# First loads put in one sequence on one DMA queue, with the last weight chunks moved to a second queue behind a wait

## The chip, the cores and the metric

The kernel runs on one core of one Trainium2 chip. The metric is the device time of one execution in microseconds (us). Executions of one kernel differ here by about 0.5% without any change, so medians are given with their range, and ratios with a 95% interval. A ratio is the mean time of one kernel's fast runs over that of the other's in the same rounds, so it is not quite the ratio of the medians beside it. The profile counts a "span" from the first to the last instruction, about 1.3 us less than the time of the same execution.

## The reference, cut to what matters

```python
x = A_x                                           # [1, 2048, 640], bf16
g = sigmoid((x * gate_w).sum(-1, keepdims=True))
qkv = x @ wqkv                                    # wqkv [640, 1920]: q, k, v of 640 columns each
pq, pk = phi(q), phi(k)                           # phi(t) = where(t > 0, t + 1, exp(t)) + 1e-6
a = linear_attention(pq, pk, v) @ wo
b = (gelu(x @ w_gate) * (x @ w_up)) @ w_down
return g * a + (1 - g) * b
```

The argument touches only the very first work: Q and K of the first row tiles of x (128 rows each). A projection sums over 640 input columns in five chunks of 128, so it needs x transposed and the five chunks of the weights wk and wq, 160 KB each.

## The kernel before

DMAs are issued from two queues, SyncE's ("sp") and ScalarE's ("act"). Tiles 0 and 1 of x are loaded plainly and transposed on TensorE; tiles 2 to 15 come by DMA transposes on SyncE's queue. The first of these waits until wk chunk 4 has landed.

```python
load_x(0)
load_wk(0)
load_x(1, "act")
load_wk(1)
load_wk(3)
# ...
load_wk(2, "act")
load_wk(4, "act")
# ... (gate weights, "act")
for k in range(KC):                       # KC = 5
    load_wq(k, ("sp", "act")[k % 2])
# ...
for i in range(NXN, NT):                  # tiles 2 to 15
    load_xT(i, after=([r_wk[4]] if i == NXN else ()))
# ... bulk loads of x and of the other weights, same queue
```

TensorE's order: warming matmuls on constants, transposes `T(tile, chunks, bank)`, then K steps `KM(n, [chunk])` and Q steps `QM(n, [chunk])` of both tiles, then `KQ(i)`, the joint K and Q projection of tiles 2 to 15.

```python
warm(5, 512); warm(1, 128)
T(0, [0], 7); T(0, [1, 2, 3, 4], 6)
warm(6, 128)
KM(0, [0])
T(1, [0], 7); T(1, [1, 2, 3, 4], 6)
warm(3, 128)
KM(1, [0])
for k in (1, 2, 3):
    KM(0, [k]); KM(1, [k])
gate_col()
for k in (4,):
    KM(0, [k]); KM(1, [k])
# ... Q of tiles 0 and 1 chunk by chunk, phi of all four results
for i in range(2, NT):
    KQ(i)
```

Of the kernel before, what the change touches and what calls it, by code (L numbers as in the profile page):

```python
# [16 lines left out]
KC = D // 128  # L17
# [6 lines left out]
NXN = 2  # L24
# [137 lines left out]
def bass_gated_mix__linear_attn_block__geglu_ffn__prompt_kernel(  # L162
# [63 lines left out]
    with (  # L226
# [8 lines left out]
        with contextlib.ExitStack() as stack:  # L235
            dma_sems = [stack.enter_context(nc.semaphore("s_in%d" % i)) for i in range(n_dma_in)]

            P = _Plan(["pe", "act", "dve", "pool", "sp"])
# [9 lines left out]
            def new_dma_key():  # L248
                k = "in%d" % dma_next[0]
                dma_next[0] += 1  # L250
                return k

            def v16(o, n):
                return pool[:, o:o + n]
# [14 lines left out]
            wq = wkq[:, :, 640:1281]  # L269
# [30 lines left out]
            gw_sb = v16(O_GW, 128)  # L300
# [8 lines left out]
            r_wk = [P.sb("wk%d" % k, R_WK + k * WW, R_WK + k * WW + 640) for k in range(KC)]  # L309
            r_wq = [P.sb("wq%d" % k, R_WK + k * WW + 640, R_WK + k * WW + 1280) for k in range(KC)]  # L310
# [26 lines left out]
            r_gw = P.res("gw")  # L337

            def dma_in(dst, src, writes, reads=(), eng="sp"):
                P.op(eng, lambda e, dst=dst, src=src: e.dma_start(dst, src),  # L340
                     reads=reads, writes=writes, dma=new_dma_key())
# [3 lines left out]
            def load_x(i, eng="sp"):  # L345
                dma_in(x_aug[:, i, 0:640], A_x[0, i * 128:(i + 1) * 128, :], [r_xn[i]], eng=eng)

            def load_wk(k, eng="sp"):
                dma_in(wk[:, k, :], A_wqkv[k * 128:(k + 1) * 128, 640:1280], [r_wk[k]], eng=eng)

            def load_wq(k, eng="sp"):
                dma_in(wq[:, k, 0:640], A_wqkv[k * 128:(k + 1) * 128, 0:640], [r_wq[k]], eng=eng)


            P.op("act", lambda e: e.dma_start(touch[0:16, 0:4], A_wqkv[0:128:8, 640:644]),
                 writes=[P.res("touch")], dma=new_dma_key())
            load_x(0)
            load_wk(0)
            load_x(1, "act")
            load_wk(1)  # L360
            load_wk(3)

            zero = nc.const_aps.tensor(0.0, (128, 1), F32)
            P.op("act", lambda e: e.activation(eg[:, 0:1], zero, ACT.Exp), writes=[r_eg[0]])
            load_wk(2, "act")
            load_wk(4, "act")
            P.op("dve", lambda e: e.memset(gw_sb, 0.0), writes=[r_gw])
            dma_in(gw_sb[0:5, :], gate_w.rearrange("(k p) -> k p", p=128), [r_gw], eng="act")
            for k in range(KC):
                load_wq(k, ("sp", "act")[k % 2])  # L370

            def load_xT(i, after=()):
                P.op("sp", lambda e: e.dma_start_transpose(xT[:, :, i * 128:(i + 1) * 128],
                                                           A_x[0, i * 128:(i + 1) * 128, :]),
                     reads=list(after), writes=[r_xT[i]], dma=new_dma_key())

            for i in range(NXN, NT):
                load_xT(i, after=([r_wk[4]] if i == NXN else ()))
            dma_in(x_aug[:, NXN:8, 0:640],
                   A_x[0, NXN * 128:8 * 128, :].rearrange("(i p) w -> p i w", p=128), r_xn[NXN:8])  # L380
            dma_in(x_aug[:, 8:NT, 0:640],
# [4 lines left out]
            for c in range(NHC):  # L386
# [9 lines left out]
                 reads=[r_ones], writes=[r_ident])  # L396
# [16 lines left out]
            def warm(count, n):  # L413
                def fn(e):
                    last = None
                    for w in range(count):
                        last = e.matmul(ps[:, 4, 0:n], one_l, one_r[:, 0:n], start=True, stop=True)
                    return last
                P.op("pe", fn, writes=[bank[4]])
# [4 lines left out]
            def slot(n):  # L424
                return SLOTS[n % 4]

            def T(i, ks, tb):
                def fn(e):
                    last = None
                    for n, k in enumerate(ks):  # L430
                        last = e.transpose(psb[:, tb, n * 128:(n + 1) * 128],
                                           x_aug[:, i, k * 128:(k + 1) * 128], ident)
                    return last
                P.op("pe", fn, reads=[r_xn[i], r_ident], writes=[bank[tb]])
                P.op("dve", lambda e: e.tensor_copy(
                    xT[:, ks[0]:ks[-1] + 1, i * 128:(i + 1) * 128],
                    psb[:, tb, 0:len(ks) * 128].rearrange("p (k s) -> p k s", k=len(ks))),
                    reads=[bank[tb]], writes=[r_xTa[i] if ks[0] == 0 else r_xT[i]])
# [4 lines left out]
            def KM(n, ks):  # L443
                i = seq[n][1]
                b0, b1 = slot(n)

                def fn(e):
                    last = None
                    for k in ks:
                        lhs = xT[:, k, i * 128:(i + 1) * 128]  # L450
                        e.matmul(ps[:, b0, :], lhs, wk[:, k, 0:512], start=(k == 0), stop=(k == KC - 1))  # L451
                        last = e.matmul(ps[:, b1, 0:128], lhs, wk[:, k, 512:640],
                                        start=(k == 0), stop=(k == KC - 1))
                    return last
                P.op("pe", fn, reads=[r_xTa[i] if i < NXN and ks == [0] else r_xT[i]] + [r_wk[k] for k in ks],
                     writes=[bank[b0], bank[b1]])
# [37 lines left out]
            def gate_col():  # L494

                P.op("pe", lambda e: e.matmul(ps[:, 7, 0:5], gw_sb, ident[:, 0:5], start=True, stop=True),
                     reads=[r_gw, r_ident], writes=[bank[7]])
                P.op("dve", lambda e: e.tensor_copy(wq[:, :, 640:641], ps[:, 7, 0:5].unsqueeze(2)),
                     reads=[bank[7]], writes=[r_gcol])
# [4 lines left out]
            warm(1, 128)  # L504
            T(0, [0], 7)
            T(0, [1, 2, 3, 4], 6)
            warm(6, 128)
            KM(0, [0])
            T(1, [0], 7)
            T(1, [1, 2, 3, 4], 6)  # L510
            warm(3, 128)
            KM(1, [0])
            for k in (1, 2, 3):
                KM(0, [k])
                KM(1, [k])
            gate_col()
            for k in (4,):
                KM(0, [k])
                KM(1, [k])
            for n in range(4):  # L520
# [42 lines left out]
            for i in range(2, NT):  # L563
                KQ(i)
                if i == 4:
                    late_constants()
            P.op("dve", lambda e: e.tensor_scalar(gg, eg, 0.5, 0.5, ALU.mult, ALU.add),
                 reads=r_eg, writes=[r_g])
            P.op("dve", lambda e: e.tensor_scalar(omg, eg, -0.5, 0.5, ALU.mult, ALU.add),
                 reads=r_eg, writes=[r_omg])  # L570
# [7 lines left out]
                 reads=[r_omg], writes=[r_od], dma=new_dma_key())  # L578
# [44 lines left out]
            def ME(g):  # L623
# [6 lines left out]
                for c in cs:  # L630
# [8 lines left out]
                 reads=r_pk[0:2], writes=[r_tmp[0]])  # L639
            for i in range(2, NT):  # L640
                P.op("dve", lambda e, i=i: e.tensor_tensor(zacc, zacc, pk[i], ALU.add),  # L641
                     reads=[r_tmp[0], r_pk[i]], writes=[r_tmp[0]])
# [283 lines left out]
```

## Time and profile before

| | before |
|---|---|
| time, median of 6 runs | 273.72 us (273.44 to 274.68) |
| span of the profiled execution | 272.2 us |
| first K step / first Q step / joint projection starts | 4.38 / 7.67 / 10.39 us |
| TensorE busy | 267.9 us, 98% |

The row to read first is TensorE's: it has work in 98% of the span, and it is not interrupted once the joint projection runs. The start of that projection is therefore the number to follow. The rest of the program takes 261.8 us from there to the end (272.2 - 10.39).

### The profile page before, as it was taken

The numbers are of one execution on the slowest core, as the hardware profiler recorded it, in microseconds if no ns is written. First come the engines' busy times: TensorE is split into PE (matmuls) and PEld (weight loads), VectorE is DVE, ScalarE is ACT, GpSimd is POOL, SyncE is SP. The second block draws the span as 40 slices with busy tenths as digits, with TensorE's granted clock in tenths as the row PEclk, the third lists the DMA queues.
The fourth block names the chain that finished last, engine by engine and source line by source line (L and its number), as shares of the span: only waits on it lengthen the run. The fifth ranks groups of instructions, "written<-read, shape, count | busy, mean of one in ns | idle before, by whom it ended". The sixth has DMA issues, their size and how long they took to land.

```text
span 272.2 us, 3426 instructions
## 1 busy us (share of the span) xinstructions
PE 267.9 (98%) x1343; PEld 128.1 (47%) x1369; DVE 141.8 (52%) x251; ACT 75.9 (28%) x132; POOL 30.0 (11%) x28
## 2 busy tenths in 40 slices
PE   8999999999999999999999999999999999999997
PEld 4555555544445444444444444444444444444444
DVE  2689898997333335999999999634110000000200
ACT  2555555210422453332222232224011122121021
POOL 5000000003140002242332421000000000000000
PEclk9999999999999999999999999999999999999999
DMA  6776999500300011612221221272031110110211
GB/s 219 176 114 124 349 402 384 119 2 19 61 16 2 23 50 51 200 28 48 27 48 30 43 50 25 60 229 96 5 79 37 41 39 19 39 41 19 58 58 41
DMA packets 42208, 23.61 MB, mean 87 GB/s; under 512 B 31567, under 2 KB 40783, under 8 KB 42063
## 3 DMA queue, kind: packets, MB, share of 16 engines
q1 hardware_dynamic: 41429, 22.56, 30.5%
q10 hardware_dynamic: 762, 0.82, 0.8%
q8 instruction: 11, 0.18, 0.3%
q14 instruction: 6, 0.05, 0.1%
HBM read 13.83 MB, written 2.63 MB: 60 GB/s over the span
## 4 chain that ended last, share of the span: by engine, by line
PE 95%; DVE 2%; DMA 1%; issue 1%; ACT 1%; SPq 0%; DVEq 0%; ACTq 0%
PE ps L697 41%; PE ps L861 23%; PE ps L536 12%; PE ps L593 6%; PE ps L840 4%; PE ps L808 2%; PE ps L675 2%; PE ps L596 2%; DMA pool<-in_A_wqkv_dram 1%; PE ps L451 1%; PE ps L821 1%; PE ps L466 1%; DVE pool L490 1%; PE ps L718 1%; DVE pool L555 1%
## 5 line engine op out<-in xcount | busy, mean ns | idle before, releaser
L697 PE MATMUL ps<-pool 128*128 128x512 bf16 x510 | 113.0, 379 | 0.5
L697 PEld LDWEIGHTS ps<-pool 128*128 128x128 bf16 x520 | 50.4, 98 | 60.1
L861 PE MATMUL ps<-pool 128*128 128x512 bf16 (+2 forms) x300 | 62.4, 367 | 0.3
L703 ACT ACTIVATE pool<-ps 128x512 f32<-128x512 f32 x52 | 31.0, 597 | 73.1 <-PE ps L697 73.1
L705 DVE TENSOR_TENSOR pool<-ps,pool 128x512 bf16<-128x512 f32 x52 | 34.6, 689 | 31.7 <-PE ps L697 30.4
L861 PEld LDWEIGHTS ps<-pool 128*128 128x128 bf16 x306 | 29.1, 98 | 33.5 <-issue 0.4
L536 PE MATMUL ps<-pool 128*128 128x512 bf16 (+1 forms) x206 | 37.9, 344 | 0.2
L844 DVE TENSOR_TENSOR pool<-ps,pool 128x512 bf16<-128x512 f32 x4 | 2.8, 692 | 61.5 <-PE ps L840 61.5
L751 POOL TENSOR_TENSOR pool<-pool 128x640 f32<-128x640 bf16 x16 | 22.5, 1406 | 72.8 <-DVE pool L753 65.9
L868 ACT ACTIVATE pool<-ps,pool 128x512 bf16<-128x512 f32 (+1 forms) x16 | 10.9, 680 | 68.6 <-PE ps L861 68.6
L536 PEld LDWEIGHTS ps<-pool 128*128 128x128 bf16 x210 | 20.5, 98 | 17.5
L555 DVE SCALAR_TENSOR_TENSOR pool<-ps,pool 128x128 bf16<-128x128 f32 (+2 forms) x42 | 25.3, 603 | 2.4
L546 ACT ACTIVATE pool<-ps 128x640 bf16<-128x640 f32 x28 | 19.7, 703 | 18.1 <-DVE pool L555 10.6
L593 PE MATMUL ps<-pool 128*128 128x512 bf16 x76 | 19.2, 380 | 0.1
L761 DVE TENSOR_TENSOR pool<-pool 128x640 bf16<-128x640 bf16 x16 | 13.2, 825 | 0.6
L759 DVE TENSOR_SCALAR pool<-pool 128x32 f32<-128x32 f32 x16 | 12.8, 803 | 0.6
L753 DVE TENSOR_REDUCE pool<-pool 128x32 f32<-128x640 f32 x16 | 12.9, 809 | 0.0
L641 DVE TENSOR_TENSOR pool<-pool 128x640 f32<-128x640 f32 x14 | 11.6, 826 | 0.5
L840 PE MATMUL ps<-pool 128*128 128x512 bf16 x51 | 11.5, 380 | 0.1
L643 POOL PARTITION_ALL_REDUCE pool<-pool x1 | 4.0, 3971 | 60.7 <-DVE pool L641 60.7
L593 PEld LDWEIGHTS ps<-pool 128*128 128x128 bf16 x78 | 6.9, 98 | 7.2
L552 DVE TENSOR_SCALAR pool<-pool 128x640 bf16<-128x640 bf16 x28 | 9.1, 327 | 1.8 <-ACT pool L546 0.4
(70 smaller groups left out, 105.0 us busy)
## 6 DMA issues: line engine op xcount, KB each, us to landing
out_dram<-pool SPq DMA_DIRECT2D x19, 128.0 KB, 1.7
pool<-in_B_w_gate_dram SPq DMA_DIRECT2D x1, 2080.0 KB, 14.2
pool<-in_B_w_up_dram SPq DMA_DIRECT2D x1, 2080.0 KB, 18.8
pool<-in_A_x_dram SPq DMA_DIRECT2D x1, 1280.0 KB, 8.7
pool<-in_B_w_down_dram SPq DMA_DIRECT2D x1, 1120.0 KB, 6.1
pool<-omg_row SPq DMA_DIRECT2D x1, 1024.0 KB, 4.8
pool<-in_A_wqkv_dram SPq DMA_DIRECT2D x6, 160.0 KB, 4.4
pool<-in_A_x_dram SPq DMA_DIRECT2D x1, 960.0 KB, 5.8
```

The source lines that it names most:

```text
L536: last = e.matmul(ps[:, b + p, 0:c1 - c0], xT[:, k, i * 128:(i + 1) * 128], wkq[:, k, c0:c1], start=(k == 0), stop=(k == KC - 1))
L546: P.op("act", lambda e: e.activation(e_buf[m], ps_flat[:, o:o + 640], ACT.Exp), reads=banks, writes=[r_e[m]])
L555: P.op("dve", lambda e, c0=c0, c1=c1: e.scalar_tensor_tensor(dst[:, c0:c1], ps_flat[:, o + c0:o + c1], 1.0 + EPS, e_buf[m][:, c0:c1], ALU. ...
L593: last = e.matmul(ps[:, b, :], pk[i][:, c * 128:(c + 1) * 128], x_aug[:, i, 0:512], start=(i == 0), stop=(i == NT - 1))
L697: last = e.matmul(ps[:, b, :], w[:, k, fc * 128:(fc + 1) * 128], xT[:, k, j * 512:(j + 1) * 512], start=(k == 0), stop=(k == KC - 1))
L703: P.op("act", lambda e: e.activation(ge[n], ps[:, gb, :], ACT.Gelu_apprx_tanh), reads=[bank[gb]], writes=[r_ge[n]])
L705: P.op("dve", lambda e: e.tensor_tensor(hT[fc][:, j * 512:(j + 1) * 512], ps[:, ub, :], ge[n], ALU.mult), reads=[bank[ub], r_ge[n]], write ...
L751: P.op("pool", lambda e: e.tensor_tensor(tmp[n], pq[i], z_b, ALU.mult), reads=[r_pq[i], r_zb], writes=[r_tmp[n]])
L753: P.op("dve", lambda e: e.tensor_reduce(den[n], tmp[n].rearrange("p (h d) -> p h d", h=32), AX.X, ALU.add), reads=[r_tmp[n]], writes=[r_de ...
L761: P.op("dve", lambda e: e.tensor_tensor(pq[i].rearrange("p (h d) -> p h d", h=32), pq[i].rearrange("p (h d) -> p h d", h=32), den[n].unsqu ...
L840: last = e.matmul(ps[:, b, :], wd[:, fc, 512:640], hT[fc][:, j * 512:(j + 1) * 512], start=False, stop=(fc == NFC - 2), skip_group_check=True)
L861: last = e.matmul(ps[:, pb, 0:c1 - c0], lhs, rhs, start=False, stop=(q == len(rows) - 1), skip_group_check=True)
```

## The change

The intent: give the early loads a fixed order, so that each K chunk arrives when it is wanted and nothing unneeded shares the DMA engines with it. All first loads go on SyncE's queue; wq chunks 2 to 4 are issued by ScalarE, but only when wk chunk 2 is in. The wait ahead of the transposes is dropped. TensorE transposes both tiles before K begins.

```diff
-            load_x(0)
-            load_wk(0)
-            load_x(1, "act")
-            load_wk(1)
-            load_wk(3)
+            load_x(0)
+            load_x(1)
+            for k in range(KC):
+                load_wk(k)
 ...
-            load_wk(2, "act")
-            load_wk(4, "act")
-            (gate weights, now second on ScalarE's queue)
-            for k in range(KC):
-                load_wq(k, ("sp", "act")[k % 2])
+            load_wq(0)
+            load_wq(1)
+            for k in (2, 3, 4):
+                load_wq(k, "act", after=[r_wk[2]])
 ...
-                load_xT(i, after=([r_wk[4]] if i == NXN else ()))
+                load_xT(i)
 ...
-            warm(6, 128)
-            KM(0, [0])
+            warm(2, 128)
             T(1, [0], 7)
-            T(1, [1, 2, 3, 4], 6)
-            warm(3, 128)
-            KM(1, [0])
-            for k in (1, 2, 3): ...   gate_col()   for k in (4,): ...
+            T(1, [1, 2, 3, 4], 5)
+            warm(4, 128)
+            for k in range(KC):
+                if k == 3:
+                    gate_col()
                 KM(0, [k])
                 KM(1, [k])
```

More of the change, by code (lines that the diff above doesn't have):

```diff
@@ L349, in load_wk, with load_wq @@
                 dma_in(wk[:, k, :], A_wqkv[k * 128:(k + 1) * 128, 640:1280], [r_wk[k]], eng=eng)
-            def load_wq(k, eng="sp"):
-                dma_in(wq[:, k, 0:640], A_wqkv[k * 128:(k + 1) * 128, 0:640], [r_wq[k]], eng=eng)
+            def load_wq(k, eng="sp", after=()):
+                dma_in(wq[:, k, 0:640], A_wqkv[k * 128:(k + 1) * 128, 0:640], [r_wq[k]], reads=after, eng=eng)
             P.op("act", lambda e: e.dma_start(touch[0:16, 0:4], A_wqkv[0:128:8, 640:644]),
                  writes=[P.res("touch")], dma=new_dma_key())
+            P.op("dve", lambda e: e.memset(gw_sb, 0.0), writes=[r_gw])
+            dma_in(gw_sb[0:5, :], gate_w.rearrange("(k p) -> k p", p=128), [r_gw], eng="act")
             load_x(0)
-            load_wk(0)
-            load_x(1, "act")
-            load_wk(1)
-            load_wk(3)
+            load_x(1)
+            for k in range(KC):
+                load_wk(k)
             zero = nc.const_aps.tensor(0.0, (128, 1), F32)
             P.op("act", lambda e: e.activation(eg[:, 0:1], zero, ACT.Exp), writes=[r_eg[0]])
-            load_wk(2, "act")
-            load_wk(4, "act")
-            P.op("dve", lambda e: e.memset(gw_sb, 0.0), writes=[r_gw])
-            dma_in(gw_sb[0:5, :], gate_w.rearrange("(k p) -> k p", p=128), [r_gw], eng="act")
-            for k in range(KC):
-                load_wq(k, ("sp", "act")[k % 2])
+            load_wq(0)
+            load_wq(1)
+            for k in (2, 3, 4):
+                load_wq(k, "act", after=[r_wk[2]])
             def load_xT(i, after=()):
@@ L506, in bass_gated_mix__linear_attn_block__geglu_ffn__prompt_kernel @@
             T(0, [1, 2, 3, 4], 6)
-            warm(6, 128)
-            KM(0, [0])
+            warm(2, 128)
             T(1, [0], 7)
-            T(1, [1, 2, 3, 4], 6)
-            warm(3, 128)
-            KM(1, [0])
-            for k in (1, 2, 3):
-                KM(0, [k])
-                KM(1, [k])
-            gate_col()
-            for k in (4,):
+            T(1, [1, 2, 3, 4], 5)
[3 more added lines that the diff above has]
+                    gate_col()
                 KM(0, [k])
```

## The prediction

> **What bounds the kernel now.** I read the page first, then the timeline of the first 18 us engine by engine, then the waits of that stretch, then each load's time to landing one window at a time.
>
> ```profile
> span 272.2 us, 3426 instructions
> PE 267.9 (98%) x1343; PEld 128.1 (47%) x1369; DVE 141.8 (52%) x251; ACT 75.9 (28%) x132; POOL 30.0 (11%) x28
> PE 95%; DVE 2%; DMA 1%; issue 1%; ACT 1%; SPq 0%; DVEq 0%; ACTq 0%
> ```
>
> The busy line and the chain that ended last say the same: TensorE sets the end, and it is free for only 272.2 - 267.9 = 4.3 us of the whole span. The change touches only the first ten microseconds, so all it can do is let TensorE's long unbroken stretch begin earlier or later. The question is where that stretch begins. The timeline of TensorE (start, length, engine, line, form, count, idle before):
>
> ```profile
> 0.82 2.40 PE L417 MATMUL ps<-const-bfloat16-1.0 128*128 128x512 bf16 x6 [0.82 <-PEq L911]
> 3.02 0.74 PE L431 MATMUL ps<-pool 128*128 128x128 bf16 x5
> 3.55 0.62 PE L417 MATMUL ps<-const-bfloat16-1.0 128*128 128x128 bf16 x6
> 4.38 0.38 PE L451 MATMUL ps<-pool 128*128 128x512 bf16 x1 [0.21 <-DMA pool<-in_A_wqkv_dram]
> 4.64 0.44 PE L431 MATMUL ps<-pool 128*128 128x128 bf16 x5
> 4.92 0.34 PE L417 MATMUL ps<-const-bfloat16-1.0 128*128 128x128 bf16 x3
> 5.18 0.39 PE L451 MATMUL ps<-pool 128*128 128x512 bf16 x1
> 5.46 0.38 PE L451 MATMUL ps<-pool 128*128 128x512 bf16 x1
> 5.74 0.38 PE L451 MATMUL ps<-pool 128*128 128x512 bf16 x1
> 7.67 0.38 PE L466 MATMUL ps<-pool 128*128 128x512 bf16 x1
> 10.39 7.85 PE L536 MATMUL ps<-pool 128*128 128x512 bf16 x40
> ```
>
> L417 is warming on constants, L431 the transposes of x tiles 0 and 1, L451 the K projection of these tiles, L466 their Q projection, L536 the joint K and Q projection of tiles 2 to 15. From 5.46 on nothing is free: a step of one tile and one chunk (512 and 128 columns) repeats every 0.27 us (5.46 to 5.74). Nine records of L466 appear where ten instructions were issued, so the small hole near 8.2 is a missing record. L536 needs 2.71 us a tile; ScalarE's first read of each comes at that interval:
>
> ```profile
> 15.46 0.70 ACT L546 ACTIVATE pool<-ps 128x640 bf16<-128x640 f32 x1 [0.45 <-PE ps L536]
> 18.17 0.70 ACT L546 ACTIVATE pool<-ps 128x640 bf16<-128x640 f32 x1 [0.46 <-PE ps L536]
> ```
>
> So the useful stretch starts at 5.46, with chunk 1, and what held it there is a load: the weight-load row at 5.45 has 0.16 us idle put down to the weight DMA. The loads themselves:
>
> ```profile
> 0.79 0.41 SPq L340 DMA_DIRECT2D pool<-in_A_x_dram  x1
> 1.26 2.78 SPq L340 DMA_DIRECT2D pool<-in_A_wqkv_dram  x6
> 6.51 19.01 SPq L373 DMA_TRANSPOSE pool<-in_A_x_dram  x14
> 1.23 0.45 ACTq L340 DMA_DIRECT2D pool<-in_A_x_dram  x1
> 1.78 0.87 ACTq L340 DMA_DIRECT2D pool<-in_A_wqkv_dram  x2
> SPq L373 <- DMA pool<-in_A_wqkv_dram: 2.5, 1, 2.5
> ```
>
> SyncE issues every (4.04 - 1.26)/6 = 0.46 us. Adding the times to landing, window by window, to the times of issue: x0 0.79+2.2 = 3.0; wk0 1.26+3.0 = 4.25; x1 1.23+3.2 = 4.4; wk1 1.71+3.7 = 5.4; wk2 1.78+3.8 = 5.6; wk3 2.18+4.1 = 6.25; wk4 2.19+4.3 = 6.5; wq0 7.4; wq1 7.8; wq2 8.25; wq4 8.9; wq3 8.95. After x1, nine loads take 4.5 us: one 160 KB load per 0.50 us. Two queues feed one supply, and wk1 waits in it beside wk2, which nobody needs yet.
>
> **What the Trainium skill says.** "DMA: Bandwidth & Descriptors", section "Issuing engines are not separate DMA queues": transfers issued from ScalarE and SyncE run on the same 16 DMA engines and interleave, and a second issuer saves only issue time. The trace agrees: the spacing of 0.50 us with two issuers is hardly longer than one issuer's 0.46 us. So one issuer should lose almost no supply, and order becomes controllable. The same page, "DMA Transpose (X-bar)" and its rules: a transpose beside ordinary loads needs no serializing, so dropping the wait for wk4 is safe; whether it costs bandwidth the page does not say for this mix. "TensorE: Matmul & The Clock Gate", section "What's actually happening": the array runs at half rate until about 3.4 us of activity, run-variably. Here the five 512-column warming matmuls take about 0.43 us each (2.40 us for five and a small one, less the overlap of ends), the step at 5.46 shows 0.21 us from L451 to L452, and by 4.38 the array is fast.
>
> **The change part by part.**
>
> Order of loads. All of x0, x1, wk0 to wk4, wq0, wq1 go at 0.46 us from 0.79: issues at 0.79, 1.26, 1.72, 2.18, 2.65, 3.11, 3.57, 4.04, 4.50. I estimate landings from before: the second load on SyncE's queue landed at 4.25 while sharing with x1, so alone about 3.6; three loads were in by 4.4 with parts of two others, so wk0 at about 4.1; then 0.50 each: wk1 4.6, wk2 5.1, wk3 5.6, wk4 6.1, wq0 6.6, wq1 7.1.
>
> TensorE's start. Both tiles are now transposed before any K step, which needs x1 (3.6). After the first transposes and two warming matmuls TensorE is at about 3.75; five transposes at about 0.09 us and four warming matmuls at 0.07 bring it to about 4.5. VectorE has by then copied chunk 0 of both tiles (0.23 us each, its queue being free at 4.2). wk0 is there. So K starts at 4.5, and with two tiles a chunk takes 0.55 us against one load per 0.50 us: chunks 1 to 4 are wanted at 5.05, 5.6, 6.15, 6.7 and are there 0.45 us earlier or more.
>
> Before, K chunk 1 began at 5.46; now at 4.5 + 0.55 = 5.05. Gain 0.41 us. The gate column is one matmul as before, only a chunk earlier, and its load, now second on ScalarE's queue instead of fifth, is early enough: 0.
>
> Q. ScalarE blocks until wk2 lands (5.1), then issues three loads at 0.44: 5.15, 5.6, 6.05. Nothing else is asked of ScalarE until the end of K near 7.25, so blocking costs 0. Q wants its chunks at 7.3, 7.85, 8.4, 8.9, 9.45. wq0 and wq1 have 0.7 us to spare. wq2 to wq4 compete with SyncE's transposes, now issued from about 4.97 instead of 6.51. By 0.50 us each after wq1 they come at 7.6, 8.1, 8.6; if transposes take a third of the supply (estimate), 7.8, 8.5, 9.2. Enough, but only by 0.25 us at the end.
>
> Transposes. The first of them came 3.7 us after issue; behind wq1 it should be there by about 9.2, and tile 2 is wanted at 10.39 - 0.41 = 9.98. They go on at 1.36 us each against 2.71 us of TensorE, so they stay ahead; the 1.5 us by which all later loads move forward wins nothing.
>
> Warming: nine small matmuls become six; they lie before the start and cost nothing beyond what is counted above.
>
> Sum: 0.41 us less, of which I keep 0.35 because the margin at wq4 is thin. 273.87 - 0.35 is 273.5 us.
>
> **Rivals.** One: the transposes take the supply from wq2 to wq4 and Q waits. For it: the margin of 0.25 us and the removed wait, which was there to keep transposes behind the weights. Against: they queue behind wq1 on SyncE, and ScalarE's loads are on their own queue. It would eat 0.2 to 0.6 us: 273.7 to 274.1. Two: one queue supplies the start more slowly (x1 near 4.1 rather than 3.6), and TensorE idles before the first K step. K then starts at 4.8 to 5.0, the gain falls to nothing: 273.8. Three: with four fewer warming matmuls between the two sets of transposes, and both sets of transposes ahead of K, the clock opens later. Up to 3 us of K steps at half rate would cost 1.5 us: 275. Against: TensorE is as busy as before from 0.82 on, and it was fast at 4.38; I give it one chance in twelve. Four: the phi work of VectorE takes the place as bound; its loop repeats with TensorE's at 2.71 us and moves along with it, so no.
>
> **Range and chances.** Three runs of before spread over 1.15 us, more than the effect. The range is the effect (-0.6 to +0.2) and half that spread: 272.8 to 274.4. A change of 2% is 5.5 us, more than TensorE's whole idle time, so faster is next to excluded; slower would need a stall that nothing here shows.
>
> **What would show it.** The first L451 near 4.5 with no idle time before it; both L451 tiles without a break; the first L466 near 7.25 (before 7.67); the first L536 near 9.97 (before 10.39); transposes issued from 5.0. An idle stretch on TensorE put down to weights during L466 is rival one; idle time before the first L451 is rival two; L451 steps of 0.5 us are rival three. The span otherwise unchanged from L536 on. If L536 starts over 0.3 us earlier and the time does not fall, noise or a later wait decides, and the argument is wrong that everything after simply shifts.

## The result, and the profile after

| | before | after |
|---|---|---|
| median of 6 runs | 273.72 us (273.44 to 274.68) | 276.66 us (275.92 to 277.55) |
| ratio of fast runs | 1 | 1.0099 (1.0071 to 1.0128) |
| span of the profiled execution | 272.2 | 274.7 |
| first K / first Q / joint projection | 4.38 / 7.67 / 10.39 | 4.83 / 8.44 / 12.94 |

The kernel became slower by 1.0%, some 2.9 us; the prediction was 0.35 us faster. The profiled execution is the fastest of the six, so it shows the smallest loss, 2.5 us. The page's own lines of the changed kernel are these:

```profile
span 274.7 us, 3446 instructions
PE 270.6 (98%) x1366; PEld 129.0 (47%) x1366; DVE 141.9 (52%) x251; ACT 76.0 (28%) x132; POOL 30.0 (11%) x28
PE 95%; DMA 3%; SPq 1%; issue 0%; ACTq 0%; DVE 0%
```

Busy times and shares look the same: averages over the span cannot show a loss of 2.5 us at its start. Only the chain does: DMA has gone from 1% to 3%. TensorE's timeline shows where (start, length, engine, line, form, count, and the idle time before with what ended it; L450 is K, L465 is Q, L531 the joint projection):

```profile
4.83 0.63 PE L450 MATMUL ps<-pool 128*128 128x512 bf16 x1
5.37 0.63 PE L450 MATMUL ps<-pool 128*128 128x512 bf16 x1
6.78 0.38 PE L450 MATMUL ps<-pool 128*128 128x512 bf16 x1
...
8.44 0.38 PE L465 MATMUL ps<-pool 128*128 128x512 bf16 x1
...
10.34 0.39 PE L465 MATMUL ps<-pool 128*128 128x512 bf16 x1 [0.65 <-DMA pool<-in_A_wqkv_dram]
...
11.82 0.39 PE L465 MATMUL ps<-pool 128*128 128x512 bf16 x1 [0.76 <-DMA pool<-in_A_wqkv_dram]
...
12.94 9.37 PE L531 MATMUL ps<-pool 128*128 128x512 bf16 x50
```

Two things are to be seen. First, the K steps begin at half rate: 4.83 to 5.37 is 0.54 us where a step takes 0.27 later. Second, Q takes 12.94 - 8.44 = 4.50 us instead of 10.39 - 7.67 = 2.72, with two holes, ahead of chunks 2 and 3, each ended by a weight load. So of the 2.55 us by which the joint projection is late, 0.77 arose before Q and 1.78 in Q. These are places, not independent causes: the last hole ended when wq chunk 3 was in, at 11.8, and a Q that had begun earlier would only have waited longer for it. From 12.94 to the end it is 274.7 - 12.94 = 261.8 us, as before: all of the loss lies in the first 13 us.

The issues of the changed kernel, from the timelines of SyncE and ScalarE:

```profile
0.79 0.88 SPq L340 DMA_DIRECT2D pool<-in_A_x_dram  x2
1.71 3.28 SPq L340 DMA_DIRECT2D pool<-in_A_wqkv_dram  x7
5.03 17.09 SPq L372 DMA_TRANSPOSE pool<-in_A_x_dram  x12
6.04 1.68 ACTq L340 DMA_DIRECT2D pool<-in_A_wqkv_dram  x3
```

ScalarE could issue its three wq loads only at 6.04, one microsecond after SyncE had issued the first transpose. The view of these three loads alone (issue time on the queue in ns, minimum, median, maximum; first and last start; then the time from issue to landing):

```profile
L340 ACTq DMA_DIRECT2D pool<-in_A_wqkv_dram x3: 356/617/647, 6.0 to 7.1; - x3
DMA to landing us min/median/max: 4.3/5.2/5.3
```

They landed at about 10.3, 11.8 and 12.3 us; Q wanted them at 9.5, 10.1 and 10.6. By comparison, the seven weight loads on SyncE's queue took 3.0 to 3.8 us each.

### The profile page after: what moved, and what is told of

Read it like the earlier page. It is cut to its first block, busy times and chain, and to the rows that moved or that the text cites.

```text
span 274.7 us, 3446 instructions
## 1 busy us (share of the span) xinstructions
PE 270.6 (98%) x1366; PEld 129.0 (47%) x1366; DVE 141.9 (52%) x251; ACT 76.0 (28%) x132; POOL 30.0 (11%) x28
## 4 chain that ended last, share of the span: by engine, by line
PE 95%; DMA 3%; SPq 1%; issue 0%; ACTq 0%; DVE 0%
PE ps L692 41%; PE ps L856 23%; PE ps L531 14%; PE ps L588 6%; PE ps L835 4%; DMA pool<-in_A_wqkv_dram 3%; PE ps L803 2%; PE ps L670 2%; PE ps L591 1%; PE ps L816 1%; SPq L340 1%; PE ps L713 1%; PE ps L731 0%; PE ps L465 0%; PE ps L598 0%; PE ps L822 0%
## 5 line engine op out<-in xcount | busy, mean ns | idle before, releaser
L531 PE MATMUL ps<-pool 128*128 128x512 bf16 (+1 forms) x210 | 38.1, 344 | 0.0
L531 PEld LDWEIGHTS ps<-pool 128*128 128x128 bf16 x210 | 20.5, 98 | 17.5
L756 DVE TENSOR_TENSOR pool<-pool 128x640 bf16<-128x640 bf16 x16 | 13.2, 824 | 0.6
```

Source lines behind the costliest of these rows:

```text
L531: last = e.matmul(ps[:, b + p, 0:c1 - c0], xT[:, k, i * 128:(i + 1) * 128], wkq[:, k, c0:c1], start=(k == 0), stop=(k == KC - 1))
L756: P.op("dve", lambda e: e.tensor_tensor(pq[i].rearrange("p (h d) -> p h d", h=32), pq[i].rearrange("p (h d) -> p h d", h=32), den[n].unsqu ...
```

## The experiments

Twelve kernels ran. In all, the result was correct. Two of them, those with all weights on SyncE's queue, were first stopped by the check before the chip: with ScalarE's weight loads gone, nothing ordered the end of the program after the tiny first load on that queue. A wait for it at the very end of the program mended that; the cuts below leave this line out.

The theories were: A, transposes ahead of ScalarE's three wq loads hold these up, in a strong form (they take from any weights in flight) and a weak one (only from loads issued behind them); B, the loads are simply issued too late; C, one queue supplies too slowly.

### The wait of the transposes put back

```diff
-                load_xT(i)
+                load_xT(i, after=([r_wk[4]] if i == NXN else ()))
```

> The changed kernel, with the first transpose again waiting for wk chunk 4. Theory A (the transposes, put ahead of ScalarE's three wq loads, hold these up): transposes start near 7.1, wq2 to wq4 land by about 9.5, Q is not interrupted for more than 0.3 us, joint projection starts at 11.2 to 11.6 instead of 12.94, time 275.0 to 275.4. Theory B (ScalarE issues too late because it waits for wk chunk 2): waits stay, joint projection at 12.3 or later, time 276.2 to 276.8. Theory C (the supply of one queue is simply too slow): as B.

Measured: 274.56 us median (274.15 to 274.88, 4 runs) against 273.85 of the kernel before in the same rounds, ratio 1.0016 (0.9996 to 1.0036). Most of the loss is gone with this one line. ScalarE's loads were issued from 5.90 instead of 6.04 and landed after 3.5 to 3.8 us instead of 4.3 to 5.3:

```profile
L340 ACTq DMA_DIRECT2D pool<-in_A_wqkv_dram x3: 356/453/455, 5.9 to 6.8; - x3
DMA to landing us min/median/max: 3.5/3.7/3.8
```

B falls as the main cause, since the issue time is nearly unchanged. The last of them was in at 10.5, though, not by 9.5 as A had said. The joint projection began at 11.74, a little later than A said, for a new reason, which its TensorE row names:

```profile
11.74 4.59 PE L531 MATMUL ps<-pool 128*128 128x512 bf16 x23 [0.35 <-DMA pool<-in_A_x_dram]
```

With the wait, tile 2 comes late: wk chunk 4 lands near 7.0 in the single sequence (6.5 and 6.9 in the two profiles of the kernel before), and the transpose is put off with it.

### All wq chunks on SyncE's queue, ahead of the transposes

```diff
-            load_wq(1)
-            for k in (2, 3, 4):
-                load_wq(k, "act", after=[r_wk[2]])
+            for k in range(1, KC):
+                load_wq(k)
```

> The changed kernel with all five wq chunks on SyncE's queue ahead of the transposes, ScalarE's queue unused. Theories A and B both: wq4 lands by about 10.1 at 0.57 us a load, Q is not interrupted, joint projection at 11.2, time 275.0 to 275.4; what is left over the kernel before (about 0.8 us at the start of Q) is the slow clock in K. Theory C: Q is still interrupted, because the supply of one queue is the same, joint projection at 12 or later.

Measured: 274.25 us (273.82 to 274.35, 4 runs), ratio 1.0002 (0.9985 to 1.002). The transposes still have no wait; they merely stand behind the weights in one queue, and the loss is gone, within the interval. The time is below the 275.0 to 275.4 that was expected. The joint projection began at 11.20, as expected, but not for the expected reason. TensorE was already fast when K began at 4.83; K waited 0.18 us for wk chunk 4, and Q did wait once:

```profile
9.56 0.39 PE L464 MATMUL ps<-pool 128*128 128x512 bf16 x1 [0.36 <-DMA pool<-in_A_wqkv_dram]
```

So C holds in part: wq chunk 2 landed only near 9.5 in this execution. That can hide a gain, but is not the loss that was found.

### The kernel before, with only its wait removed

```diff
-                load_xT(i, after=([r_wk[4]] if i == NXN else ()))
+                load_xT(i)
```

> The kernel before with the one wait removed: the first transpose no longer waits for wk chunk 4, issued near 4.05 behind wq4 on SyncE's queue. Theory A in its strong form (transposes take the supply from whatever weights are in flight): wq1 and wq3 on ScalarE's queue land 1 us or more later, Q is interrupted, time 274.5 to 275.5. Theory A in its weak form (only loads issued after the transposes are held up; here all weights are issued before them): no change in Q, 273.4 to 274.0.

Measured: 273.98 us (273.63 to 274.9, 4 runs), ratio 1.0001 (0.9977 to 1.0025). Dropping the wait costs nothing beyond the interval where all weights are issued before the transposes; the time favours the weak form of A. The profiled execution was the slowest of the four; in it K chunk 1 had to wait until 6.82, while Q was not interrupted. Its wq chunks 1 and 3 landed at 8.95 and 9.98, 1 us later than in the first profile of the kernel before, as the strong form said. But with the same loads and no transpose before 8.0 (the run with TensorE's new order, below) they landed at 8.86 and 9.66, so one profile does not show that the transposes, queued from 4.08, had a hand in it.

### ScalarE's wq loads issued at once

```diff
-                load_wq(k, "act", after=[r_wk[2]])
+                load_wq(k, "act")
```

> The changed kernel, with ScalarE issuing wq2 to wq4 at once, no wait for wk chunk 2. Theories A (weak) and B: these loads are ahead of the transposes, Q is not interrupted; but they now share with x1 and wk, so K starts later or is interrupted (wk0 near 5.0, wk4 near 7.7); joint projection at 11.0 to 11.8, time 274.8 to 275.6. Theory A in its strong form and C: Q is still interrupted, 276 or more.

Measured: 276.0 us (275.17 to 277.88, 4 runs), ratio 1.0088 (1.004 to 1.0136). The kind of effect was foreseen, its size was not: Q ran without a hole from 9.83 to 12.56, but K had three.

```profile
5.68 0.39 PE L450 MATMUL ps<-pool 128*128 128x512 bf16 x1 [0.71 <-DMA pool<-in_A_wqkv_dram]
7.29 0.39 PE L450 MATMUL ps<-pool 128*128 128x512 bf16 x1 [0.89 <-DMA pool<-in_A_wqkv_dram]
8.74 0.39 PE L450 MATMUL ps<-pool 128*128 128x512 bf16 x1 [0.18 <-DMA pool<-in_A_wqkv_dram]
```

Weights that nobody needs yet, on the second queue, take from the ones that K is waiting for: wk chunk 1 landed at 7.2 instead of 5.3. (The slowest of the four runs, 277.88, also has a mean clock of 0.994, as in the second profile of the changed kernel below; the other three have 275.17 to 276.46.) So the wait for wk chunk 2 in the change does serve its purpose; issuing earlier (what B asks for) only moves the waits from Q to K.

### No transpose until wq chunk 4 is in

```diff
-                load_xT(i)
+                load_xT(i, after=([r_wq[4]] if i == NXN else ()))
```

> The changed kernel with every transpose waiting until wq chunk 4 has landed, so ScalarE's three loads meet no transpose at all. Theory A (transposes in flight hold up these loads): the three land 3.0 to 3.8 us after issue, as loads do elsewhere, the last by about 10, and Q runs with less than 0.4 us of waits; but the first transpose is issued near 10 and tile 2 comes near 12.5, so TensorE waits there instead; joint projection at 12.3 to 13. Theory B or C (late issue, or a slow supply by itself): the three loads still take over 4.3 us, the last lands at 11 or later.

Measured: 277.23 us (278.17 and 276.29), ratio 1.0114 (1.0068 to 1.0159): slow, as it had to be, since tile 2 now comes late and the joint projection began at 13.41. The run is for the loads:

```profile
L340 ACTq DMA_DIRECT2D pool<-in_A_wqkv_dram x3: 356/453/455, 5.9 to 6.8; - x3
DMA to landing us min/median/max: 3.6/3.6/3.7
```

With no transpose beside them the three loads need 3.6 us, against a median of 5.2 in the changed kernel, with the same queue, the same wait and nearly the same issue. The last was in at about 10.4; Q waited 0.49 us. Tile 2 landed at 13.3.

### The same bytes untransposed in the place of three transposes

```diff
+            for i in (2, 3, 4):
+                load_x(i)
             for i in range(NXN, NT):
-                load_xT(i)
+                load_xT(i, after=([r_wq[4]] if i == NXN else ()))
```

(The later bulk load of x then starts at tile 5.)

> As the run before it, but SyncE issues plain loads of x tiles 2, 3 and 4 where the first three transposes stood: the same 480 KB, at the same place, untransposed. If the hold-up is only that 480 KB more come out of one supply: at 0.5 to 0.6 us per 160 KB the six loads alternate, ScalarE's last lands about 1.0 to 1.5 us later than in the run without them, near 11.3. If it is particular to transposes: later by 0.6 us at most, near 10.5, against 12.33 with the transposes.

Measured: 277.56 us (277.37 and 277.76), ratio 1.0126 (1.0102 to 1.015), slow for the same reason as the run before. The loads:

```profile
L340 ACTq DMA_DIRECT2D pool<-in_A_wqkv_dram x3: 356/453/464, 6.3 to 7.2; - x3
DMA to landing us min/median/max: 4.1/4.3/4.4
```

The last landed at about 11.3, 1.0 us after the run without traffic, as the expectation for a shared supply said; but 0.4 of this is later issue (6.30 instead of 5.92). From issue on, 480 KB of plain loads cost a load beside them some 0.7 us, close to the bound of 0.6 that the other expectation gave, so this run alone does not decide.

### A single transpose ahead of the wq loads

```diff
-                load_xT(i)
+                load_xT(i, after=([r_wq[4]] if i == NXN + 1 else ()))
```

> The changed kernel with only the transpose of tile 2 issued at once and tiles 3 to 15 waiting for wq chunk 4. If each transpose holds up the load beside it: wq2 comes late, near 9.4 to 10, wq3 and wq4 follow 0.5 us apart, the last by 11; joint projection at about 11.7, time 274.7 to 275.3. If one transpose is enough to hold up all three: last near 12, joint projection at 12.7, time 276 or more.

Measured: 275.54 us (274.86 to 276.09, 4 runs), ratio 1.0044 (1.0021 to 1.0067), between the changed kernel and the one with the wait put back. The profiled execution:

```profile
L340 ACTq DMA_DIRECT2D pool<-in_A_wqkv_dram x3: 356/454/455, 5.8 to 6.7; - x3
DMA to landing us min/median/max: 5.4/5.5/5.5
```

One transpose moves 160 KB, a third of the plain loads above, yet in this execution each of the three loads took 5.4 to 5.5 us; the last came at 12.1 and the joint projection began at 13.02. The second expectation fits the profile; the time lies between the two, nearer the first. By its span (274.8 us) the profiled execution was the slowest of the four. The spans of the others, 273.6 to 274.5, less the fixed 261.8 us, put the joint projection at 11.8 to 12.7 (an estimate), so one transpose costs on average less than all of them. But here it delayed the loads beside it by 1.9 us (5.5 - 3.6), and three times its bytes, untransposed, by 0.7 us.

The packets of the three loads tell the two kinds of delay apart. ScalarE's queue is q10 in the view of DMA queues; each line gives packets, MB, and the time that the packets took as a share of 16 engines over a window around the three loads. In this order: no transposes (window 7 to 10.4 us), plain loads (8 to 11.4), one transpose (7 to 12), the changed kernel (8 to 12.4).

```profile
q10 hardware_dynamic: 432, 0.49, 47.2%
q10 hardware_dynamic: 432, 0.49, 41.1%
q10 hardware_dynamic: 432, 0.49, 60.4%
q10 hardware_dynamic: 432, 0.49, 61.1%
```

Share times 16 times the window is the packets' own time in total: 26, 22, 48 and 43 us. The same 432 packets take about twice as long beside transposes, and no longer than usual beside plain loads, which only bring them later. So in these profiles the hold-up is a matter of transposes, not only of bytes. Why a packet takes longer is not shown.

### The loads of before with TensorE's new order

```diff
-            warm(6, 128)
-            KM(0, [0])
+            warm(2, 128)
             T(1, [0], 7)
-            T(1, [1, 2, 3, 4], 6)
-            warm(3, 128)
-            KM(1, [0])
+            T(1, [1, 2, 3, 4], 5)
+            warm(4, 128)
 ... (then K of both tiles chunk by chunk, as in the change; the loads as before)
```

> The loads of the kernel before with TensorE's new order (both tiles transposed before any K step). If the new order by itself costs time (a later switch to full rate, or K held by x tile 1): K starts near 5.2 and the joint projection 0.3 us or more after that of the kernel before (10.39 and 11.33 in its two profiles), time 274.2 to 275. If the loads alone decide: within noise of before, 273.6 to 274.2.

Measured: 274.33 us (273.82 to 276.14, 4 runs), ratio 1.0019 (0.9973 to 1.0064): inconclusive, one run of the four being 1.8 us above the median. K began at 5.53, behind the transposes of x tile 1, and the joint projection at 11.33, as in the second profile of the kernel before.

### One sequence with TensorE's old order

```diff
-            load_wq(1)
-            for k in (2, 3, 4):
-                load_wq(k, "act", after=[r_wk[2]])
+            for k in range(1, KC):
+                load_wq(k)
 ...
-            warm(2, 128)
+            warm(6, 128)
+            KM(0, [0])
             T(1, [0], 7)
-            T(1, [1, 2, 3, 4], 5)
-            warm(4, 128)
+            T(1, [1, 2, 3, 4], 6)
+            warm(3, 128)
+            KM(1, [0])
 ... (then the K steps in the order of the kernel before)
```

> All loads in one sequence on SyncE's queue, wq included, ahead of the transposes, with TensorE's order of the kernel before. Against the same loads with the new order (274.25, ratio 1.0002): if TensorE's order does not matter, 273.8 to 274.5, because wq chunk 2 lands at 9.5 and holds Q either way; if the new order is what makes the single sequence break even, 274.7 or more.

Measured: 274.14 us (273.96 to 274.36, 4 runs), ratio 0.9998 (0.998 to 1.0016), joint projection at 11.02. TensorE's order does not matter within the interval. The reason that was expected did not show: wq chunk 2 landed at 8.9, not 9.5, and Q ran without a hole from 8.30.

### A try at a better version

```diff
-                load_wq(k, "act", after=[r_wk[2]])
+                load_wq(k, "act", after=[r_wk[0]])
 ...
-                load_xT(i)
+                load_xT(i, after=([r_wk[4]] if i == NXN else ()))
```

> A try at a better version: the changed kernel with the wait of the transposes for wk chunk 4 put back and ScalarE's three loads issued already when wk chunk 0 has landed (near 4.8, not 5.9). The two queues then share from about 6, wq4 lands by about 9.4 instead of 10.4, Q runs with less than 0.3 us of waits, joint projection at 10.9 to 11.3, time 273.7 to 274.3. If the shared supply delays wk3 and wk4 as much as it brings wq forward: no better than 274.5.

Measured: 274.61 us (274.28 to 274.92, 4 runs), ratio 1.0015 (0.9994 to 1.0035). The joint projection began at 11.25. It fails, as the second expectation said: wq chunk 4 came at 10.0, earlier, but wq chunk 0, now sharing, at 8.4, and the first Q step waited 0.50 us for it. No version that ran beats the kernel before beyond its interval.

### The kernel before and the changed kernel, each profiled once more

> The kernel before once more, for its profile: whether the switch of TensorE to full rate (before 4.38 us in the first profile) comes at the same time in every execution. If it is free of the program, it moves by up to 3 us between executions and the joint projection starts at 10.4 to 11.5; if the order of TensorE's work sets it, it stays before 4.4 and the start at 10.4.

Measured: 274.41 us, span 273.2, joint projection at 11.33, not 10.39; TensorE was fast at its first K step. What differed was the supply: that step waited for its weights until 5.32.

```profile
5.32 0.38 PE L451 MATMUL ps<-pool 128*128 128x512 bf16 x1 [1.17 <-DMA pool<-in_A_wqkv_dram]
```

The profile on which the prediction rests was a lucky execution (273.55 us, at the low end of the runs): the first loads of the same program can be 1 us later.

> The changed kernel once more, for its profile. If the hold-up by the transposes is in every execution: the last wq load lands over 5 us after issue, near 12 or later, and the joint projection starts at 12.5 to 14. The switch to full rate, at 6.45 us in the first profile, should be elsewhere, between 3.5 and 6.9.

Measured: 278.57 us, span 277.2, the slowest run of all. The three wq loads took 5.2, 5.5 and 6.5 us, the last landing at about 13.3. In addition TensorE fell back to half rate, as the windows show (stretch, its length, busy time and instruction count of PE, PEld, DVE, ACT and POOL, then granted TensorE clock, DMA share, GB/s):

```profile
10.00:11.00 1.00, 0.00 (x0) 0.00 (x0) 0.97 (x3) 0.00 (x0) 0.00 (x0) 1.00 1.19 253
...
12.00:13.00 1.00, 0.49 (x4) 0.15 (x2) 0.00 (x0) 0.00 (x0) 0.00 (x0) 1.00 1.45 140
13.00:14.00 1.00, 0.70 (x3) 0.39 (x4) 0.00 (x0) 0.00 (x0) 0.00 (x0) 0.61 1.14 244
14.00:15.00 1.00, 1.00 (x5) 0.41 (x3) 0.21 (x1) 0.94 (x3) 0.00 (x0) 0.50 1.03 208
15.00:16.00 1.00, 1.00 (x3) 0.30 (x2) 0.89 (x3) 0.48 (x2) 0.00 (x0) 0.50 0.52 100
16.00:17.00 1.00, 1.00 (x5) 0.40 (x4) 0.90 (x3) 0.00 (x0) 0.00 (x0) 0.68 0.71 137
```

From about 13.2 to 16.6 the clock is halved, after holes of 1.36 and 0.81 us in Q. From the start of the joint projection at 14.35 to the end it is 262.9 us, 1.1 more than elsewhere. The first run with no transpose until wq chunk 4 was in had the same (13.41 to the end of 276.8, 263.4 us, mean clock 0.994). So a hole in this place can be paid twice, but need not be: in the changed kernel's first profile it was not, nor with plain loads, where the holes were 1.29 and 1.79 us and the rest took 261.7; nor is a halved clock recorded for any of the changed kernel's six timed runs, whose mean clock is 1.0.

## Why the prediction was wrong, point by point

**What bounds, and what a shift is worth: right.** The end follows the start of the joint projection at a fixed 261.7 to 261.9 us in before, after and every other profile but two, in which TensorE's clock fell back for 3 us.

**Order of loads: the rate was mis-sized.** The prediction took 0.50 us a load, the spacing of landings in one execution, and expected it of one queue because that queue issues every 0.46 us; an interval of issue was compared with a spacing of landings. In the changed kernel x1 landed at 3.75 (predicted 3.6), wk0 at 4.7 (4.1), wk2 at 6.0 (5.1), wk4 at 7.1 (6.1), wq1 at 8.4 (7.1): wk0 was 0.6 us late, and the six loads after it took 3.6 us, 0.60 each. With no transpose near them wk4 came at 7.2 and wq1 at 8.1, so the transposes are not the main reason. That the single queue is the reason is not shown either: from two queues the nine loads after x1 landed 0.50 and 0.42 us apart in the two profiles of the kernel before, but 0.61 (4.55 to 10.03) with the same loads and TensorE's new order.

**TensorE's start: off by 0.33 us.** K began at 4.83, not at 4.5, with no idle time before it: warming matmuls at half rate ran until then. Full rate would have brought little, as wk0 was in only at 4.74; in the single sequence, where TensorE was fast by then, it waited for wk0 and began at 4.83 too. This is rival two by half: the loads were late, x1 hardly. Half rate until about 6.6 (rival three, at one chance in twelve) made four steps take 6.78 - 4.83 = 1.95 us instead of four times 0.273. It delayed Q's start, but not the joint projection, since Q had to wait for its weights in any case. In the nine other profiles with TensorE's new order it became fast by 3.8, 4.1, 4.3, 4.8, 5.2, 5.6, 6.1, 6.4 and 6.6 us; with the old order, between 3.6 and 5.4 in four. Executions differ in it; whether the new order shifts it on average is not shown.

**Q: the step that failed.** The prediction said "if transposes take a third of the supply (estimate), 7.8, 8.5, 9.2. Enough, but only by 0.25 us at the end." They came at 10.3, 11.8 and 12.3. Two errors add up. ScalarE issued at 6.04 instead of 5.15, because wk chunk 2 landed 0.9 us later than supposed; even with no transpose beside them (issue from 5.92) the three came at 9.6, 10.0 and 10.4, with a hole of 0.5 us in a Q that began at 7.86. The changed kernel's Q wanted them at 9.5, 10.1 and 10.6, so this error alone would have cost it little. The larger one is the share of a third, for which the prediction had no trace: behind a transpose these loads take a median of 5.2 us instead of 3.6. Rival one was the right mechanism, at 0.2 to 0.6 us the wrong size. Putting back the one wait takes the ratio from 1.0099 to 1.0016; putting the weights ahead of the transposes in one queue takes it to 1.0002.

**Two sums were off as well.** A third taken from the supply makes 0.75 us of 0.50, so the three would come at 7.85, 8.6 and 9.35, with 0.1 us to spare, not 0.25. And 273.87 with -0.6 to +0.2 and half of 1.15 us on either side gives 272.7 to 274.6, not 272.8 to 274.4.

**The argument against rival one was the wrong way round.** "They queue behind wq1 on SyncE, and ScalarE's loads are on their own queue": the separate queue is what let the transposes get ahead. In one queue the weights would have stood before them.

**Transposes: right.** Tile 2 was in at 9.0 (predicted 9.2) and TensorE never waited for a transpose. It was the one that nobody needed early.

**The gain: not seen, and not excluded.** Without the hold-up, in the single-sequence versions, the time equals that of before (1.0002 and 0.9998), but the intervals reach down to 0.9985 and 0.998, and the predicted 0.35 us would be 0.9987. The profiles show no gain for K: Q began at 7.95 and 8.30 there, against 7.67 and 8.61 in the two profiles of before.

## What to carry to other kernels

When a wait is dropped from a queue, look for loads on the other queue that will be issued after its next entry: here those issued behind a transpose landed after 4.3 to 6.5 us instead of 3.6, and with all weights ahead of the transposes the loss was gone. Do not take the rate of supply from one execution: the same loads landed 0.42, 0.50 and 0.61 us apart in three. Profile the kernel before twice when the argument rests on tenths of a microsecond. Here a wait of TensorE at the start cost its full length, since nothing later made up for it (a fixed 261.8 us), and in two profiles here a stretch of halved clock on top, 1.1 and 1.6 us.

## What the Trainium skill lacked or had wrong

- "DMA: Bandwidth & Descriptors", section "Rules for kernel authors", says that a transpose next to ordinary DMAs needs nothing. For correctness every run agrees. For time it lacks that a 160 KB load issued within about 2 us behind a DMA transpose on the other queue landed after 4.3 to 6.5 us instead of 3.6, while 480 KB of plain loads in the same place made it 4.1 to 4.4.
- "TensorE: Matmul & The Clock Gate", section "What's actually happening", says that the point of the switch to full rate varies by about half a microsecond, though it also reports 6, 11 or 14 slow matmuls for one kernel. Here it came between 3.8 and 6.6 us of the span in ten profiles with the same order of TensorE's work and its first matmul always at 0.82 or 0.83 us.
- The same page, section "HAM oscillation — how this bites in real kernels", gives the rule of no idle gap over about 3.4 us. In the second profile of the changed kernel the clock fell to half after gaps of 1.36 and 0.81 us with four steps of Q between them.
- No page says how the granted clock is to be read where a profile has no record of it. In the kernel before the view gives 1.00 from 1 to 3 us, while the spacing of the matmuls (0.43 against 0.21 us for 512 columns) shows half rate; the first clock record of this trace begins at 3.77 us, where the spacing changes.
